# Tile shapes of the scores, the experts' results and the long turns, and the planner's booking of loads, in a fused attention and expert kernel

## The chip, the cores and the metric

One core of one Trainium2 chip. The metric is the time of one execution on the device in microseconds. Three executions of the kernel before took 511.32, 512.01 and 514.26 us (median 512.01); the profiled execution took 510.98 us, with 509.2 us from its first to its last instruction.

## What is computed

Two layers, all in float32. The first is attention with a window of 32 around each local query plus 32 global keys, and 32 global queries that see every key; 8 batches, 8 heads, 512 local and 32 global positions, head size 64. Cut to its core:

```python
s_g   = scale * q_g @ concat(k_g, k_l).T ;  out_g = softmax(s_g) @ concat(v_g, v_l)
s_ll  = where(|i - j| <= 32, scale * q_l @ k_l.T, -1e9)
out_l = softmax(concat(scale * q_l @ k_g.T, s_ll)) @ concat(v_g, v_l)
x     = concat(out_g, out_l), heads side by side          # [8, 544, 512]
```

The second is four causal attention "experts" on x, each of width 64, of which every position takes the two with the largest logits, weighted:

```python
logits = x @ w_gate ; top 2 of 4, softmax over the two -> gate
for e in range(4):
    q, k, v = x @ wq[e], x @ wk[e], x @ wv[e]
    out += gate[e] * (softmax(causal(scale * q @ k.T)) @ v @ wo[e])
```

## The kernel before, in words

Work comes in 32 pairs of heads (8 batches of 4 pairs). For a pair, `p1_load` and `p1_load_values` fetch keys, queries and values; `p1_trans` turns keys and queries (for the first four pairs by TensorE, line 523, afterwards on VectorE, lines 533 to 536) into `kd` and `qp`; GpSimd copies values into window order (`move`, lines 480 to 500, recorded at line 277) and the global keys into `kd` (line 515). `p1_scores` (line 553) takes local scores: 32 products on tiles of 64 rows and 32 columns, one PSUM bank per half of the rows. `p1_softmax` (565, 568) follows, `p1_ptrans` turns the probabilities, `p1_av` (616) multiplies with values on 128x32 tiles, `p1_turn` turns the result into x. For two pairs together `p1_global_scores` (678) takes the 32 global queries of four heads against all keys, on 128x64 tiles: the queries of two heads stand in a block-diagonal buffer (`qgbd`, cleared at the start), so that all 128 rows hold one product. `p1_global_turn` turns the probabilities, `p1_global_av` (731) multiplies.

Per batch come the projections `m_qk` (761) and `m_v` (798, 809) on full 128x128 tiles, the gates, and for each of two pairs of experts `c`: `m_scores` (890) on 64x64 tiles in three blocks of 384, 384 and 512 columns, `m_softmax` (904, 908, 922), `m_ptrans`, and `m_av` (957) on 128x64 tiles; `m_out` (1037) multiplies with wo. The last 32 positions, the "tail", of all four experts go together: `m_tail_scores` (979) on 128x64 tiles with a block-diagonal `qtbd`, `m_tail_turn`, `m_tail_av` (1018).

Two ways of turning stand in the code. `turn_halves` (586) turns a block as two tiles of 64 rows and 128 columns, each half into a bank of its own, and copies each bank out with one copy. `long_turn` (709), for the global and the tail probabilities, turns whole 128x128 blocks: four blocks into one bank, then a fifth into another, with two or three copies out.

A product of float32 operands is recorded as two matmul instructions (32 products of line 553 are 64 instructions); turns and products of float32r operands are one.

The order is not written out: `step(s)` lists the operations of a step with a priority of 100 s, and `Plan.place` simulates the engines with the costs that each `op` names and emits the instructions in that simulated order. Each engine then runs its own list in order. On TensorE the planner takes, of the ready operations within 130 of the lowest priority, the one with the smallest start time + 300 ns if its `shape` label differs from the last one's + 4 ns per unit of priority; the labels are local, quarter (expert scores), half (global and tail scores, experts' results), av, turn, and none for full tiles. A load books 700 ns and its own transfer time on one simulated DMA clock and counts as landed 1100 ns later; at most 8 loads are under way. These times exist only in the planner: on the chip an instruction waits for its data and its buffer alone. Loads are issued from SP's queue, and at priorities under 100 from ScalarE's too.

In `step`, the local part (`local`) follows the turns from step 6 on; global scores come earlier in the step, after the products with values; tail scores follow the first experts' results; long turns are spread among the full-tile products by `whole`. `setup(kind)` loads the weights of a kind (line 393 on) and splits them on VectorE (405, 407); values' weights at step 1.

## Time and profile before

| | before |
|---|---|
| executions, us | 511.32, 512.01, 514.26 |
| profiled execution, us | 510.98 |
| its span, us | 509.2 |
| TensorE busy, us (share) | 477.3 (94%) |
| TensorE weight loads, us | 405.2 (80%) |
| VectorE busy, us | 393.4 (77%) |
| ScalarE busy, us | 329.7 (65%) |
| GpSimd busy, us | 283.8 (56%) |
| instructions | 23800, of them 9564 matmuls |
| mean granted clock of TensorE | 0.989 |

Busy time is the time in which an engine had at least one instruction under way; matmuls overlap, so the time that a block takes on TensorE is read from its start to the start of the next block, not from a mean duration. The granted clock is the share of 2.4 GHz that TensorE was given.

### The profile page before, as it was taken

The numbers are of one execution on the slowest core, as the hardware profiler recorded it, in microseconds if no ns is written. First come the engines' busy times: TensorE is split into PE (matmuls) and PEld (weight loads), VectorE is DVE, ScalarE is ACT, GpSimd is POOL, SyncE is SP. The second block draws the span as 40 slices with busy tenths as digits, with TensorE's granted clock in tenths as the row PEclk, the third lists the DMA queues.
The fourth block names the chain that finished last, engine by engine and source line by source line (L and its number), as shares of the span: only waits on it lengthen the run. The fifth ranks groups of instructions, "written<-read, shape, count | busy, mean of one in ns | idle before, by whom it ended". The sixth has DMA issues, their size and how long they took to land.

```text
span 509.2 us, 23800 instructions
## 1 busy us (share of the span) xinstructions
PE 477.3 (94%) x9564; PEld 405.2 (80%) x9564; DVE 393.4 (77%) x1738; ACT 329.7 (65%) x1208; POOL 283.8 (56%) x521
## 2 busy tenths in 40 slices
PE   5687789999999998999999999999999999999995
PEld 3566778698877897789887898789886988889764
DVE  7697788997968896598987797598986797476480
ACT  1687357876957566595867666686768683553562
POOL 7886967878365673748358481838529220431220
PEclk9799899999999999999999999999999999999999
DMA  9977786443344513553243612644222000200102
GB/s 183 169 132 143 123 151 123 93 82 73 63 94 123 104 24 61 139 91 71 45 94 111 124 21 43 171 88 86 45 53 84 4 3 3 85 1 2 68 19 103
DMA packets 190190, 41.92 MB, mean 82 GB/s; under 512 B 185472, under 2 KB 185472, under 8 KB 190080
## 3 DMA queue, kind: packets, MB, share of 16 engines
q1 hardware_dynamic: 179040, 30.00, 32.6%
q10 hardware_dynamic: 11040, 10.41, 6.5%
q8 instruction: 75, 1.23, 1.1%
q14 instruction: 35, 0.29, 0.2%
HBM read 31.47 MB, written 8.91 MB: 79 GB/s over the span
## 4 chain that ended last, share of the span: by engine, by line
PE 76%; POOL 7%; DVE 6%; DMA 6%; issue 3%; ACT 2%; ACTq 1%; SPq 0%; POOLq 0%; DVEq 0%
PE bank L761 18%; PE bank L586 8%; PE bank L798 8%; PE bank L890 7%; PE bank L1037 7%; PE bank L957 6%; PE bank L553 5%; PE bank L616 5%; POOL v L277 5%; PE bank L678 3%; DMA v<-in_v_l_dram 2%; PE bank L709 2%; PE bank L731 2%; DMA kn<-in_k_l_dram 2%; PE bank L809 2%
## 5 line engine op out<-in xcount | busy, mean ns | idle before, releaser
L922 POOL TENSOR_SCALAR pm<-pm,msm,gate 128x512 f32<-128x512 f32 (+3 forms) x125 | 75.0, 614 | 115.1 <-DVE msm L913 63.9
L277 POOL COPY v<-v 32x512 f32<-32x512 f32 (+1 forms) x192 | 116.9, 609 | 31.7 <-DMA v<-in_v_l_dram 22.4
L568 ACT ACTIVATE st<-st,sm 128x128 f32<-128x128 f32 x256 | 99.3, 391 | 12.7 <-DVE sm L565 12.4
L277 POOL COPY v<-vg 32x640 f32<-32x640 f32 (+1 forms) x96 | 65.2, 680 | 45.7 <-PE bank L731 33.2
L908 ACT ACTIVATE pm<-pm,msm 128x512 f32<-128x512 f32 (+3 forms) x128 | 70.8, 555 | 16.3 <-DVE msm L904 14.0
L904 DVE CUSTOM_DVE_ANT_0 pm<-bank,cmask 128x512 f32<-128x512 f32 (+3 forms) x128 | 56.0, 483 | 12.8 <-PE bank L890 11.6
L565 DVE CUSTOM_DVE_ANT_0 st<-bank,band 128x128 f32<-128x128 f32 x256 | 56.9, 280 | 0.1
L568 ACT ACTIVATION_READ_ACCUMULATOR st<-st,sm 128x1 f32 x256 | 48.4, 189 | 0.0
L890 PE MATMUL bank<-kt,qt 64*64 64x384 f32 (+3 forms) x512 | 42.7, 442 | 0.8 <-issue 0.4
L553 PEld LDWEIGHTS bank<-kd,qp 64*32 64x32 f32 x2048 | 29.5, 107 | 17.5 <-issue 5.5
L553 PE MATMUL bank<-kd,qp 64*32 64x128 f32 x2048 | 39.1, 278 | 0.9 <-issue 0.7
L761 PE MATMUL bank<-xh,wk_hi 128*128 128x272 f32 x128 | 39.1, 305 | 0.3 <-DVE xn L620 0.2
L957 PE MATMUL bank<-mptw,vt 128*64 128x128 f32 x640 | 39.1, 275 | 0.2 <-DVE mptw L277 0.2
L798 PE MATMUL bank<-wv_hi,xl 128*128 128x260 f32 x128 | 36.3, 283 | 2.2 <-DVE xl L654 2.2
L761 PE MATMUL bank<-xh,wq_hi 128*128 128x272 f32 x128 | 38.1, 298 | 0.0
L798 PE MATMUL bank<-wv_hi,xh 128*128 128x260 f32 x128 | 37.4, 292 | 0.0
L761 PE MATMUL bank<-xl,wk_hi 128*128 128x272 f32 x128 | 37.3, 291 | 0.0
L761 PE MATMUL bank<-xh,wk_lo 128*128 128x272 f32 x128 | 37.3, 291 | 0.0
L761 PE MATMUL bank<-xl,wq_hi 128*128 128x272 f32 x128 | 36.9, 288 | 0.0
L761 PE MATMUL bank<-xh,wq_lo 128*128 128x272 f32 x128 | 36.9, 288 | 0.0
L957 PEld LDWEIGHTS bank<-mptw,vt 128*64 128x64 f32 x640 | 35.2, 137 | 1.9 <-issue 0.6
L616 PE MATMUL bank<-v,ptw 128*32 128x64 f32 x2048 | 35.9, 221 | 0.5 <-ACT ptw L275 0.3
(164 smaller groups left out, 1301.7 us busy)
## 6 DMA issues: line engine op xcount, KB each, us to landing
out_dram<-ot ACTq DMA_DIRECT2D x32, 256.0 KB, 2.1
v<-in_v_l_dram SPq DMA_DIRECT2D x62, 120.0 KB, 3.0
kn<-in_k_l_dram SPq DMA_DIRECT2D x112, 64.0 KB, 2.5
qn<-in_q_l_dram SPq DMA_DIRECT2D x112, 64.0 KB, 2.5
v<-in_v_l_dram SPq DMA_DIRECT2D x30, 64.0 KB, 3.1
vg<-in_v_g_dram SPq DMA_DIRECT2D x22, 64.0 KB, 2.9
kn<-in_k_l_dram SPq DMA_DIRECT2D x5, 128.0 KB, 4.0
ot<-in_q_g_dram SPq DMA_DIRECT2D x8, 64.0 KB, 2.5
```

The source lines that it names most:

```text
L277: ENG[e].tensor_copy(out, in_)
L553: nc.tensor.matmul(sp[h].t[32 * g:32 * g + 32, 128 * t:128 * t + 128], qp.t[rows, 32 * u:32 * u + 32], kd.t[rows, c:c + 128], start=True, ...
L565: op("DVE", 211, lambda e, h=h, t=t, i=i: nc.vector.tensor_tensor_reduce(out=st.t[:, h, t], in0=sp[h].t[:, 128 * t:128 * t + 128], in1=ban ...
L568: op("ACT", 385, lambda e, h=h, t=t, i=i: nc.scalar.activation(st.t[:, h, t], st.t[:, h, t], AF.Exp, bias=sm.t[:, 0, i:i + 1], scale=-1.0, ...
L616: nc.tensor.matmul(xq.t[32 * g:32 * g + 32, t, h, :], pt.t[:, h, 32 * u:32 * u + 32], v.t[:, h, window(u), :], start=True, stop=True)
L761: nc.tensor.matmul(pp.t, w[:, ch, cols], x(part, ch)[:, n], start=(ch == 0 and w is hi and part == 0), stop=(ch == NCH - 1 and part == 1))
L798: nc.tensor.matmul(pv.t, x(part, ch)[:, 128 * i:128 * i + 128], w[:, ch, :], start=(ch == 0 and part == 0 and w is hi), stop=(ch == NCH - ...
L890: nc.tensor.matmul(sp[x].t[64 * u:64 * u + 64, at:at + n], qt.t[rows, q0:q0 + 64], kt.t[rows, :n], start=True, stop=True)
L904: op("DVE", 78 + 1.04 * n, lambda e, x=x, at=at, n=n, i=i, s=s: nc.vector.tensor_tensor_reduce(out=pm.t[:, x, at:at + n], in0=sp[x].t[:, a ...
L908: op("ACT", 280 + 0.83 * n, lambda e, x=x, at=at, n=n, s=s: nc.scalar.activation(pm.t[:, x, at:at + n], pm.t[:, x, at:at + n], AF.Exp, bia ...
L922: lambda e, x=x, at=at, n=n, i=i, s=s: ENG[e].tensor_scalar(pm.t[:, x, at:at + n], pm.t[:, x, at:at + n], sm.t[:, 3, s:s + 1], gate.t[:, i ...
L957: nc.tensor.matmul(yp.t[64 * x:64 * x + 64, 128 * i - n0:128 * i - n0 + 128], vt.t[:, j, 64 * (2 * c + x):64 * (2 * c + x) + 64], flat[:, ...
```

## The change

Expert scores, global scores and tail scores are cut into tiles of 64 rows and 32 columns, with the label "scores" that local scores get too; experts' results into tiles of 128 rows and 32 columns, with the label "av". Queries of global rows and of the tail are read in place, so the block-diagonal buffers, their clears and the copies into them go. Long turns become one call of `turn_halves` on five blocks, into two banks, with two copies out; they stand among the turns of the step instead of among the full-tile products. Tail scores and global scores move to the head of the local part. In the planner a load may start only when at most 2000 ns of transfers are booked ahead, and it counts as landed 1600 ns after its transfer instead of 1100. The weights of values are set up a step later, and the first half of each weight's split may go to ScalarE. The diff, cut to its core:

```diff
 LANES = 8
+AHEAD = 2000.0
+LAND = 1600.0
...
-                        t = max(t, lanes[0])
+                        t = max(t, lanes[0], dma - AHEAD)
                     s = self.slot_time(o.bufs)
...
                 dma = max(dma, end + 700.0) + o.packets
-                seen = dma + 1100.0
+                seen = dma + LAND
                 lanes = lanes[1:] + [seen]
...
-    qgbd = []
-    for i in range(2):
-        t = const.tile([128, NP, 64], F32, name=f"qgbd{i}")
-        nc.vector.memset(t, 0.0)
-        qgbd.append(t)
-    qg_ring = Ring(2, fixed=qgbd)
-
-    qtbd = []
-    for i in range(2):
-        t = const.tile([128, 2, 64], F32, name=f"qtbd{i}")
-        nc.vector.memset(t, 0.0)
-        qtbd.append(t)
-    qt_ring = Ring(2, fixed=qtbd)
-
-
     def window(u):
...
         for cut, part, n in parts:
-            op("DVE", 100 + 0.6 * n, lambda e, cut=cut, part=part: nc.vector.tensor_copy(cut(hi), part()), r=[raw],
+            op("ACT|DVE", (150 + 0.83 * n, 100 + 0.6 * n), lambda e, cut=cut, part=part: copy(e, cut(hi), part()), r=[raw],
                w=[("w", kind)])
...
         op("PE", 390, f, r=[gn], w=[pg], shape="turn")
-        kg = buf("kg", [128, NP, SG])
-        qb = Buf(qg_ring)
-        evac(lambda: kg.t, lambda: pg.t[:, :, :32], 128, [pg], [kg])
-        for h in range(2):
-            rows = slice(64 * h, 64 * h + 64)
-            evac(lambda rows=rows, h=h: qb.t[rows, :, 32 * h:32 * h + 32], lambda rows=rows: pg.t[rows, :, 32:], 128,
-                 [pg], [(qb, h)])
-        G[b].update(kg=kg, qb=qb)
+        kq = G[b]["kq"] = buf("kq", [128, NP, 2 * SG])
+        evac(lambda: kq.t, lambda: pg.t, 256, [pg], [kq])
...
         pr = PR[k]
-        kg = G[b]["kg"]
+        kq = G[b]["kq"]
         kn, qn = pr["kn"], pr["qn"]
...
         op("POOL", 380, lambda e: nc.gpsimd.tensor_copy(
-            groups(kd.t)[:, :, 96:], kg.t[:, p:p + 1, :].to_broadcast([128, n3, SG])), r=[kg], w=[(kd, "g")])
+            groups(kd.t)[:, :, 96:], kq.t[:, p:p + 1, :SG].to_broadcast([128, n3, SG])), r=[kq], w=[(kd, "g")])
         if k < FIRST:
...
                                          start=True, stop=True)
-        op("PE", 990, f, r=[qp, kd], w=sp, shape="local")
+        op("PE", 990, f, r=[qp, kd], w=sp, shape="scores")
...
-        qb = G[b]["qb"]
+        kq = G[b]["kq"]
         sg = buf("long", [128, 640])
...
             def f(e, half=half, sp=sp):
-                for j in range(2):
-                    p, kd, o_ = 2 * g + j, kdl[j].t, sp.t[64 * j:64 * j + 64]
-                    if half == 0:
-                        parts = [(o_[:, :128], kd[:, :128]),
-                                 (o_[:, 128:].rearrange("p (c s) -> p c s", s=96),
-                                  kd[:, 128:512].rearrange("p (c s) -> p c s", s=128)[:, :, :96])]
-                    else:
-                        parts = [(o_[:, :96], kd[:, 512:608]), (o_[:, 96:], kd[:, 640:])]
-                    for to, k_ in parts:
-                        nc.tensor.matmul(to, qb.t[:, p, :], k_, start=True, stop=True)
-            op("PE", 754 - 520 * half, f, r=[qb, *kdl], w=[sp], shape="half")
+                for k in range(2):
+                    for j in range(2):
+                        for h in range(2):
+                            rows = slice(64 * h, 64 * h + 64)
+                            kd, o_ = kdl[j].t[rows], sp.t[64 * j + 32 * h:64 * j + 32 * h + 32]
+                            if half == 0:
+                                to, k_ = [(o_[:, :128], kd[:, :128]),
+                                          (o_[:, 128:].rearrange("p (c s) -> p c s", s=96),
+                                           kd[:, 128:512].rearrange("p (c s) -> p c s", s=128)[:, :, :96])][k]
+                            else:
+                                to, k_ = [(o_[:, :96], kd[:, 512:608]), (o_[:, 96:], kd[:, 640:])][k]
+                            nc.tensor.matmul(to, kq.t[rows, 2 * g + j, SG:], k_, start=True, stop=True)
+            op("PE", 754 - 520 * half, f, r=[kq, *kdl], w=[sp], shape="scores")
             op("DVE", 78 + 1.04 * n, lambda e, sp=sp, half=half, n=n: nc.vector.tensor_scalar(
...
-    def long_turn(src, key, where, part, chunks):
-
-        some = chunks[4:] if part else chunks[:4]
-        n = len(some)
-        pa = ps([128, n, 128], "pga")
-        if part == 0:
-            where[key] = buf("longt", [128, 5, 128])
-        pt = where[key]
-
-        def f(e):
-            for j, (at, rows) in enumerate(some):
-                nc.tensor.transpose(pa.t[:rows, j, :], src.t[:, at:at + rows], ident)
-        op("PE", 110 * n, f, r=[src], w=[pa])
-        rows = min(rows for _, rows in some)
-        evac(lambda: pt.t[:rows, 4 * part:4 * part + n, :], lambda: pa.t[:rows], 128 * n, [pa], [(pt, part)])
-        if rows < 128:
-            evac(lambda: pt.t[rows:, 0, :], lambda: pa.t[rows:, 0, :], 128, [pa], [(pt, "g")])
-
-    def p1_global_turn(b, g, part):
-        long_turn(G[b, g]["sg"], "pt", G[b, g], part, CHUNKS)
+    def long_turn(src, key, where, starts):
+
+        pt = where[key] = buf("longt", [128, 5, 128])
+        turn_halves([lambda at=at: src.t[:, at:at + 128] for at in starts], [src], into(lambda: pt.t, pt, 5))
+
+    def p1_global_turn(b, g):
+        long_turn(G[b, g]["sg"], "pt", G[b, g], [at for at, _ in CHUNKS])
...
         evac(lambda: t.t[:, n], lambda: pp.t, HS, [pp], [(t, half)])
-        if kind == "q" and half == 1:
-            if c == 0:
-                M[b, "qt"] = Buf(qt_ring)
-            qt = M[b, "qt"]
-            for x_ in range(2):
-                rows = slice(64 * x_, 64 * x_ + 64)
-                evac(lambda rows=rows, x_=x_: qt.t[rows, c, 32 * x_:32 * x_ + 32],
-                     lambda rows=rows: pp.t[rows, HS - SG:], 32, [pp], [(qt, (c, x_))])
...
                 n = 128 * (i + 1)
-                for u in range(2):
+                for u in range(4):
                     for x in range(2):
                         rows = slice(64 * x, 64 * x + 64)
-                        q0 = 128 * i + 64 * u
-                        nc.tensor.matmul(sp[x].t[64 * u:64 * u + 64, at:at + n], qt.t[rows, q0:q0 + 64],
+                        q0 = 128 * i + 32 * u
+                        nc.tensor.matmul(sp[x].t[32 * u:32 * u + 32, at:at + n], qt.t[rows, q0:q0 + 32],
                                          kt.t[rows, :n], start=True, stop=True)
-        op("PE", 80 + 1.67 * sum(128 * (i + 1) for i, _ in TILES[t]), f, r=[kt, qt], w=sp, shape="quarter")
+        op("PE", 80 + 1.67 * sum(128 * (i + 1) for i, _ in TILES[t]), f, r=[kt, qt], w=sp, shape="scores")
...
                     for j in range(i + 1):
-                        for x in range(2):
-                            nc.tensor.matmul(yp.t[64 * x:64 * x + 64, 128 * i - n0:128 * i - n0 + 128],
-                                             vt.t[:, j, 64 * (2 * c + x):64 * (2 * c + x) + 64],
-                                             flat[:, where[x, i, j], :], start=(j == 0), stop=(j == i))
+                        for d in range(4):
+                            nc.tensor.matmul(yp.t[32 * d:32 * d + 32, 128 * i - n0:128 * i - n0 + 128],
+                                             vt.t[:, j, 128 * c + 32 * d:128 * c + 32 * d + 32],
+                                             flat[:, where[d // 2, i, j], :], start=(j == 0), stop=(j == i))
             op("PE", 214 * sum(i + 1 for i in some), f, r=[vt, *{id(pts[i][0]): pts[i][0] for i in some}.values()], w=[yp],
-               shape="half")
+               shape="av")
             high_low(lambda part, n0=n0, n=n: y[part].t[:, c, n0:n0 + n], lambda yp=yp: yp.t, n, [yp],
...
     def m_tail_scores(b):
-        qt = M[b, "qt"]
         gt = M[b, "gt"]
         kts = [M[b, c, "k"] for c in range(2)]
+        qts = [M[b, c, "q"] for c in range(2)]
         pm = buf("long", [128, 640])
...
             def f(e, n0=n0, n=n, sp=sp):
-                for c in range(2):
-                    nc.tensor.matmul(sp.t[64 * c:64 * c + 64], qt.t[:, c, :], kts[c].t[:, n0:n0 + n], start=True, stop=True)
-            op("PE", 30 + 1.67 * n, f, r=[qt, *kts], w=[sp], shape="half")
+                for z in range(E):
+                    c, rows = z // 2, slice(64 * (z % 2), 64 * (z % 2) + 64)
+                    nc.tensor.matmul(sp.t[32 * z:32 * z + 32], qts[c].t[rows, SL:], kts[c].t[rows, n0:n0 + n],
+                                     start=True, stop=True)
+            op("PE", 30 + 1.67 * n, f, r=[*qts, *kts], w=[sp], shape="scores")
             if half == 0:
...
-    def m_tail_turn(b, part):
-        long_turn(M[b, "ptail"], (b, "pttail"), M, part, [(128 * j, 128) for j in range(5)])
+    def m_tail_turn(b):
+        long_turn(M[b, "ptail"], (b, "pttail"), M, [128 * j for j in range(5)])
...
         def local():
+            if r == 1 and has(old):
+                m_tail_scores(old)
+            if at(s) and s % 2 == 1:
+                bb, p = PAIRS[s]
+                p1_global_scores(bb, p // 2)
             if at(s):
...
                 whole_turns.append(M[old, "turn"])
-        if at(s) and s % 2 == 1:
-            bb, p = PAIRS[s]
-            p1_global_scores(bb, p // 2)
         if r == 1 and has(old):
             m_av(old, 0)
-            m_tail_scores(old)
         if r == 3 and has(old):
...
             turns.append(lambda: sooner(s - 2, p1_turn))
+        if at(s - 1) and s % 2 == 0:
+            turns.append(lambda: p1_global_turn(PAIRS[s - 1][0], PAIRS[s - 1][1] // 2))
+        if r == 2 and has(old):
+            turns.append(lambda: m_tail_turn(old))
         if at(s + 1):
...
-        if at(s - 1) and s % 2 == 0:
-            bb, p = PAIRS[s - 1]
-            whole_turns += [lambda: p1_global_turn(bb, p // 2, 0), lambda: p1_global_turn(bb, p // 2, 1)]
-        if r == 2 and has(old):
-            whole_turns += [lambda: m_tail_turn(old, 0), lambda: m_tail_turn(old, 1)]
         if s == LAG - 1:
...
         step(s)
-        for name, when in (("masks", 3), ("v", 1), ("k", 3), ("q", 4), ("o", 6)):
+        for name, when in (("masks", 3), ("v", 2), ("k", 3), ("q", 4), ("o", 6)):
             if s == when:
```

## Rows read from the trace of the kernel before

**Rows 1.** Busy time of each engine by stretch of the span, with instruction counts

```profile
0.00:12.73 12.73, 6.53 (x97) 4.69 (x99) 9.16 (x45) 2.33 (x6) 9.18 (x31) 1.00 1.11 183
12.73:25.46 12.73, 8.82 (x188) 7.07 (x193) 7.98 (x48) 7.70 (x34) 11.32 (x19) 0.73 0.97 169
25.46:38.20 12.74, 11.09 (x431) 8.49 (x419) 12.70 (x60) 11.05 (x49) 10.89 (x21) 1.00 0.70 132
38.20:76.40 38.20, 30.99 (x687) 27.77 (x688) 30.08 (x123) 20.21 (x83) 28.37 (x46) 0.96 0.79 139
76.40:490.00 413.60, 406.89 (x8043) 347.11 (x8041) 328.40 (x1451) 281.51 (x1024) 221.88 (x404) 1.00 0.33 70
490.00:509.20 19.20, 13.00 (x140) 10.11 (x140) 5.04 (x16) 6.85 (x17) 2.16 (x4) 0.97 0.20 69
```

**Rows 2.** Timeline of TensorE at the head of one batch

```profile
212.32 1.53 PE L890 MATMUL bank<-kt,qt 64*64 64x128 f32 x24
213.77 1.16 PE L553 MATMUL bank<-kd,qp 64*32 64x128 f32 x64
214.86 1.10 PE L616 MATMUL bank<-v,ptw 128*32 128x64 f32 x64
215.89 1.09 PE L890 MATMUL bank<-kt,qt 64*64 64x512 f32 x8
216.91 1.16 PE L553 MATMUL bank<-kd,qp 64*32 64x128 f32 x64
```

**Rows 3.** Timeline of TensorE, middle of the same batch

```profile
224.49 0.71 PE L586 MATMUL bank<-ident,st 64*128 64x64 f32 x16
225.04 0.91 PE L586 MATMUL bank<-ident,pm 64*128 64x64 f32 x24
225.79 0.41 PE L586 MATMUL bank<-ident,xn 64*128 64x64 f32 x8
...
226.62 1.10 PE L616 MATMUL bank<-v,ptw 128*32 128x64 f32 x64
227.54 0.75 PE L731 MATMUL bank<-v,longt 128*32 128x64 f32 x40
228.22 1.23 PE L678 MATMUL bank<-kd,qgbd 128*64 128x128 f32 x16
229.22 2.43 PE L957 MATMUL bank<-mptw,vt 128*64 128x128 f32 x40
231.44 1.17 PE L979 MATMUL bank<-kt,qtbd 128*64 128x512 f32 x8
232.53 0.71 PE L586 MATMUL bank<-ident,st 64*128 64x64 f32 x16
```

**Rows 4.** Timeline of TensorE, the first block of the next batch

```profile
270.48 0.88 PE L890 MATMUL bank<-kt,qt 64*64 64x384 f32 x8
```

**Rows 5.** Timeline of TensorE, a long turn between other blocks

```profile
247.22 0.66 PE L709 MATMUL bank<-ident,long 128*128 128x128 f32 x4
247.63 0.37 PE L761 MATMUL bank<-xh,wk_hi 128*128 128x272 f32 x1
```

**Rows 6.** Instructions on the tile of tail queries: ns least, median, most

```profile
L275 ACT COPY qtbd<-bank x25: 178/180/181, 66.6 to 471.8; 64x32 f32<-64x32 f32 x25
```

**Rows 7.** Timeline of TensorE at the start, waits in brackets

```profile
13.34 0.66 PE L523 MATMUL bank<-ident,kn 128*128 128x128 f32 x4 [0.31 <-DMA kn<-in_k_l_dram]
17.59 1.09 PE L523 MATMUL bank<-ident,qn 128*128 128x128 f32 x4 [3.60 <-DMA qn<-in_q_l_dram]
18.61 1.96 PE L553 MATMUL bank<-kd,qp 64*32 64x128 f32 x64
...
47.93 0.39 PE L798 MATMUL bank<-wv_hi,xh 128*128 128x260 f32 x1
```

**Rows 8.** Timeline of ScalarE's queue at the start

```profile
9.77 2.15 ACTq L293 DMA_DIRECT2D qn<-in_q_l_dram  x2
```

**Rows 9.** Timeline of VectorE at the start

```profile
25.18 0.68 DVE L405 CAST wv_hi<-mptw 128x1024 fp32r<-128x1024 f32 x1
```

## The prediction

> **What bounds the kernel now.** I read the busy time by stretch first, then TensorE's own order in one batch, then the start. TensorE is busy 477.3 of 509.2 us, and by stretch the kernel has three parts [rows 1]. From 76.40 to 490.00 TensorE is busy 406.89 of 413.60 us, so only 6.7 us of that stretch is waiting: whatever shortens TensorE's own work there shortens the kernel almost one for one. Up to 76.40 it is idle for 6.2, 3.9, 1.7 and 7.2 us of the four stretches, 19.0 us together, and there the chain of loads, copies and softmax decides. The last 19.20 us hold 13.00 us of TensorE and a drain of results. The other engines leave room after 76.40 (VectorE 328.40 of 413.60), but not before: from 25.46 to 38.20 VectorE has 12.70 of 12.74 us.
>
> In the middle the reader should look at what a change of tile shape costs. The local values' product (line 616, 128x32 tiles) takes 0.92 us to the next start where a product of the same shape follows (226.62 to 227.54), and 1.03 us where expert scores on 64x64 tiles follow (214.86 to 215.89) [rows 2, 3]. The instructions are the same 64, so the change of shape costs 0.11 us. Whole products lose about as much; I take 0.105 us a change. In the batch from 212.32 to 270.48 I count 25 changes of shape [rows 2, 4]; 7.1 such batches of 58.16 us fill the 413.60 us.
>
> **The change part by part, against the profiled execution's own 510.98 us** (its span 509.2; the median of the three runs is 1.0 us higher, far inside what I leave open).
>
> *Fewer shapes.* Expert scores (line 890), global scores (678) and tail scores (979) take the local scores' 64x32; experts' results (957) take the values' 128x32. In the batch of the rows, four pairs of neighbours become one shape: expert scores and the local scores behind them (212.32 with 213.77, and 215.89 with the next at 216.91, twice per batch). The two runs of 128x64 (global scores, experts' results, tail scores, 228.22 to 232.53) dissolve: the results join the products of values ahead of them, and the global and tail scores, now issued in the step's local part, join a run of scores. That is 6 of 25. 7.1 x 6 would be 43; the first and last batches hold fewer such neighbours, and relabelling every block in the order after 76.40 this way, long turns put among the other turns, removes 39: 39 x 0.105 = 4.1 us. With fewer classes the planner, which pays 300 ns in its cost for a change, can regroup once more per batch: 7 batches x 0.105 = 0.7 us. Bounds: 20 x 0.105 = 2.1 us (only the expert/local pairs) to 55 x 0.105 = 5.8 us.
>
> *Twice the instructions in these blocks.* Expert scores stream the same columns on eight tiles instead of four. The nearest rows: local scores stream 4 x 128 columns by 64 instructions in 1.09 us (213.77 to 214.86), expert scores 512 columns by 8 in 1.02 us (215.89 to 216.91) [rows 2]; 56 more instructions add 0.07 us, 1.25 ns each. The change adds at most 24 to a block (24 to 48), so 0.03 us; 48 blocks of (8 batches, 2 pairs of experts, 3 tiles) would add 0.5 us with 8 each as the least. I take +0.5, bounds 0 to 48 x 0.07 = 3.4. Experts' results take 2.22 us for 40 instructions (229.22 to 231.44) [rows 3], 0.055 us each, two side by side; four side by side on 128x32 need 80 instructions, and line 616 starts one in 0.92/64 = 0.014 us, so 1.15 us of issue lies under 2.22 us of streaming: 0, bounds 0 to 16 x 40 x 1.25 ns = 0.8 us. Global and tail scores get the same treatment: 0, if the rival below doesn't hold.
>
> *Long turns in row halves.* Now four blocks in 0.41 us (247.22 to 247.63) [rows 5] and the fifth by itself, hardly more than its issue. After: ten instructions of the row-half turns, of which 24 take 0.75 us (225.04 to 225.79) and 16 take 0.55 us (224.49 to 225.04) [rows 3], so 0.31 to 0.34 us. Of the 24 (two per batch for global rows, one for the tail) some 20 lie after 76.40: at the 0.06 us between the lower of these and the middle, 20 x 0.06 = 1.2 us off TensorE, if they sit in a run of turns; at worst each opens a run of its own, +2.1. Their evacuations go from three copies (two for the tail) to two of 320 columns. The 32 copies into the masked tail queries go (25 on ScalarE at 0.18 us, so 5.8 us in all [rows 6]), as do two of three copies per batch turn and four clears at the start. I count all that as 0 after 76.40, where both engines wait for TensorE; were they the bound there, the 5.8 us would be worth half of it each.
>
> *Loads.* The two new numbers enter only the planner's clock (a load waits there until no more than 2 us of transfers are booked; landing is taken 0.5 us later). No instruction waits for them on the chip: they alter the order on SP's and ScalarE's queues and, through the expected landings, TensorE's order. What the order of before does wrong is visible: line 523 turns pair 2's keys at 13.34, then waits 3.60 us for pair 2's queries, and pair 1's local scores, whose keys and queries had been turned already, stand behind it until 18.61 [rows 7]. The late transfer was issued from ScalarE's queue between 9.77 and 11.92 [rows 8], behind values. The scores then show 1.96 us instead of the 1.16 of the same 64 instructions at 213.77: the granted clock of that stretch is 0.73 [rows 1, 2, 7], part of it on the 1.2 GHz level, after this idle time. With values held back and landings expected later, pair 1's scores should go ahead of that turn. Value weights move a step (some 6 us) later, past pair 4's keys and queries and pair 3's values on SP, which so come a weight's issue earlier; the weights are wanted at 47.93 [rows 7] and their first cast stands at 25.18 [rows 9], so the delay lies under over 15 us of other work; without that cover it would cost its 6 us. Casts that may go to ScalarE relieve VectorE just where it is full. Of the 19 us idle before 76.40 I take -3.0 us: the 3.6 us wait, less what VectorE keeps. Bounds: -6 (wait, slow clock and part of VectorE's queue) to +3 (another load late in its turn).
>
> *New waits.* The row-half long turn needs two PSUM banks at once, where it had one; global and tail scores stand earlier in their step, and in TensorE's fixed order everything queues behind a block whose keys or banks are late; softmax on VectorE and ScalarE waits behind that. The middle has 6.7 us of waits now. I take +1.0, bounds -1 to +4.
>
> Sum: 510.98 - 4.1 - 0.7 + 0.5 - 1.2 - 3.0 + 1.0 = 503.5; toward the median of runs, **504.0 us**.
>
> **Rivals.**
> *Row halves in one bank take turns (slower).* Global and tail scores had all 128 rows in one tile; now rows 0 to 63 and 64 to 127 are separate tiles that write into one bank, on different 32 partitions. In the kernel of before every helper that splits rows (local and expert scores, turns) gives each half a bank of its own, so no row shows this case. If the halves exclude each other, each block streams its columns twice: 16 global blocks by another 1.00 us (228.22 to 229.22) and 8 tail blocks by another 1.0 (231.44 to 232.53 without the change) [rows 3], +24 us, giving 528. It decides from the point where 8 of these 24 blocks double. Against it: the partitions are disjoint, and the four column groups already run side by side in line 616. Chance 0.10. The Trainium skill bears on this: "TensorEngine Tiling (Array Packing)", Gotcha 1 (PSUM Pressure), says that different row tiles cannot access one PSUM bank at the same time, and does not say whether different partitions are exempt. By that rule the sum is the 528 of this rival; no run here shows it yet.
>
> *The order hardly changes.* The planner may keep scores apart because their banks or inputs come at different times, and the start may stay: -2.1 - 1.2 + 0.5 + 0.5 from the middle and 0 from the start give 508.7, with new waits up to 512. For it: two runs of scores with a run of values between them (212.32 to 215.89) already serve one step each. Chance 0.16.
>
> *The start moves as a whole.* Pair 1's softmax five us earlier pulls pairs 2 to 5 along, -6: 501, or 498 with the low ends of the middle. Against it: VectorE is full from 25.46 to 38.20. Chance 0.10.
>
> *New waits at their upper bound with a late load:* 504 + 3 + 6 = 513, chance 0.02 slower, 0.02 the same.
>
> **How the numbers follow.** The forecast has 0.60 with 499 to 508 of its own. A measurement of this kernel tells about 0.5% (2.6 us) from no change, so faster means below 509.4, slower above 514.6. Faster: 0.60 + 0.10 + 0.06 of the order rival = 0.76; same: 0.10 of it + 0.02 = 0.12; slower: 0.10 + 0.02 = 0.12. The range 496.5 to 511.5 leaves out the bank rival and the ends of the others.
>
> **What would show it.** Right: 64x32 scores back to back, about 17 to 19 changes of shape in a batch of about 57 us, TensorE still busy over 97% from 76 to 490; 0.3 us per long turn; pair 1's local scores before 15 us. Wrong: global scores at 2 us a block or second-half instructions that start only when the first half ends (bank rival); a middle stretch with over 10 us of idle TensorE; the same 3.6 us wait at line 523.

## The result, and the profile after

The change makes the kernel slower: 516.71 us median of 20 executions (512.45 to 520.71) against 512.28 us of 20 executions of the kernel before on the same chip, ratio 1.0075 with a 95% interval of 1.0053 to 1.0097. Ratios, here and below, are of fast executions alone, without two of the 20 here (520.18 and 520.71) that count as slow, so they are not quite those of the medians. The profiled execution took 519.15 us, 517.4 from first to last instruction, 8.2 us more than before. The forecast was 504.0.

The busy time by stretch, in the columns of [rows 1] (length, then busy time and instructions of TensorE, its weight loads, VectorE, ScalarE, GpSimd; granted clock, DMA share, GB/s):

```profile
0.00:12.73 12.73, 6.16 (x69) 4.66 (x77) 9.45 (x39) 1.84 (x3) 10.63 (x32) 1.00 1.02 176
12.73:25.46 12.73, 10.36 (x337) 8.68 (x322) 10.32 (x63) 9.88 (x43) 11.24 (x22) 1.00 0.82 149
25.46:38.20 12.74, 9.01 (x377) 6.90 (x365) 11.21 (x48) 9.26 (x41) 6.98 (x12) 1.00 0.64 123
38.20:76.40 38.20, 30.72 (x710) 27.56 (x711) 29.12 (x113) 19.92 (x77) 27.55 (x48) 0.82 0.85 149
76.40:490.00 413.60, 393.98 (x9328) 347.11 (x9335) 317.77 (x1414) 267.08 (x965) 223.69 (x405) 0.99 0.33 70
490.00:517.40 27.40, 20.08 (x373) 15.51 (x371) 11.87 (x45) 12.22 (x35) 3.47 (x6) 0.92 0.19 66
```

The fifth line decides. TensorE is idle for 413.60 - 393.98 = 19.6 us of that stretch, where it was idle for 6.7 [rows 1]. No other engine became the bound: VectorE and ScalarE are busy for 10.6 and 14.4 us less. What TensorE waited for in that stretch (total, times, longest):

```profile
PE bank L982 <- issue: 6.0, 3, 2.0
PE bank L919 <- issue: 4.4, 3, 2.1
PE bank L597 <- DVE msm L866: 2.9, 6, 0.6
PE bank L701 <- issue: 2.0, 2, 1.7
PE bank L597 <- issue: 1.4, 1, 1.4
PE bank L567 <- issue: 0.7, 2, 0.5
PE bank L534 <- issue: 0.6, 1, 0.6
PE bank L567 <- DVE msm L866: 0.6, 1, 0.6
PE bank L661 <- issue: 0.4, 1, 0.4
```

"issue" means that nothing in the profile released the instruction: no semaphore, engine or load. I call these untraced waits; here they are 15.5 us, in the kernel before 2.9, of which these are 2.4 (the other two are of 0.3 and 0.2 us):

```profile
PE bank L1018 <- issue: 1.5, 2, 1.4
...
PE bank L678 <- issue: 0.5, 1, 0.5
...
PE bank L890 <- issue: 0.4, 1, 0.4
```

They sit inside blocks, not between them. TensorE's timeline around one (start, length, line, tile, count; in brackets the idle time and what ended it):

```profile
200.27 1.19 PE L661 MATMUL bank<-kd,kq 64*32 64x128 f32 x32
202.06 1.10 PE L597 MATMUL bank<-v,ptw 128*32 128x64 f32 x64 [0.60 <-DVE msm L866]
202.95 0.77 PE L701 MATMUL bank<-v,longt 128*32 128x64 f32 x40
203.51 0.54 PE L982 MATMUL bank<-vt,longt 128*32 128x64 f32 x23
206.03 0.69 PE L982 MATMUL bank<-vt,longt 128*32 128x64 f32 x17 [1.98 <-issue]
206.47 3.82 PE L919 MATMUL bank<-mptw,vt 128*32 128x128 f32 x80
```

The tail's values (982) stop after 23 of their 40 products, for 1.98 us, with all their inputs there. Such a stop comes once in each of five batches, at 144, 204, 264, 324 and 384 us, in the run values (597), global values (701), tail values (982), experts' results (919): 64 + 40 + 40 + 80 products in a row (products are counted here and below as recorded, two for each float32 product). In the other half of a batch the run lacks the tail's 40, and it passes without a stop at 174, 234, 294 and 354 us (not at 116); the one at 294:

```profile
294.25 1.10 PE L597 MATMUL bank<-v,ptw 128*32 128x64 f32 x64 [0.46 <-DVE msm L866]
295.16 0.75 PE L701 MATMUL bank<-v,longt 128*32 128x64 f32 x40
295.73 2.37 PE L919 MATMUL bank<-mptw,vt 128*32 128x128 f32 x80
```

A stop costs more than itself when the clock falls behind it. The 80 products of line 919 take 3.82 us at 206.47 and 2.37 at 295.73; the granted clock right behind the stop (the third number from the end) is 0.50, the 1.2 GHz level:

```profile
206.03:209.20 3.17, 3.17 (x69) 3.17 (x72) 0.81 (x5) 0.40 (x2) 0.90 (x2) 0.50 0.67 149
```

After 76 us this happened behind two of the five stops (the second at 266.35, where line 919 took 3.58 us), some 1.3 us each. Behind the stop that ended at 146.59 the same block took 2.36, and why the clock fell behind some stops only is not shown.

What is late during such a stop is the instructions themselves. The third part of the page counts the transfers that bring them; queue 8, before and after:

```profile
q8 instruction: 75, 1.23, 1.1%
```

```profile
q8 instruction: 87, 1.43, 1.1%
```

1.43 MB in 87 packets is 16 KB a packet. TensorE ran 11156 products after and 9564 before, each with one weight load, 22312 and 19128 instructions; 87 x 256 = 22272 and 75 x 256 = 19200. So one packet is 256 of TensorE's instructions, 128 products with their loads, 64 bytes each. The Trainium skill gives that size too, in "Trainium Architecture — The Big Picture", section "The software stack"; that section has the streams carried into the engines when the program is loaded, while this trace shows TensorE's arriving throughout the run.

In the trace's transfers the packet ahead of the stop above starts at 203.14 and has landed at 204.69; the stop ends at 206.03. Each of the five long stops ends 1.3 to 1.5 us after a packet has landed. Counting products shows that this is no coincidence. From each of these stops to the next TensorE does 1402, 1402, 1402 and 1403 products, and 11 packets land each time, 11 x 128 = 1408. All untraced waits of 0.2 us and more behind the first 10 us, 15 in this trace and 157 in all 14 kept traces, stand on this grid: 128 products for each packet that has landed, plus a rest that only falls, from 88 near the start to 49 near the end in this trace (about 100 other instructions of TensorE stand in between). So each of them stands where the delivered products are used up and one more packet has just come in.

### The profile page after: what moved, and what is told of

Its sections match the earlier page's. It is cut to its first block, busy times and chain, and to the rows that moved or that the text cites. A ratio compares the mean times of both kernels' runs of the same rounds, so it can differ in the third digit from the quotient of the medians.

```text
span 517.4 us, 26911 instructions
## 1 busy us (share of the span) xinstructions
PE 470.3 (91%) x11156; PEld 410.4 (79%) x11156; DVE 389.7 (75%) x1718; ACT 320.2 (62%) x1160; POOL 283.6 (55%) x521
## 3 DMA queue, kind: packets, MB, share of 16 engines
q8 instruction: 87, 1.43, 1.1%
## 4 chain that ended last, share of the span: by engine, by line
PE 74%; DVE 8%; DMA 6%; issue 5%; SPq 4%; POOL 1%; ACT 1%; ACTq 1%; POOLq 0%; DVEq 0%
PE bank L731 18%; PE bank L567 9%; PE bank L1001 9%; PE bank L760 8%; PE bank L919 7%; PE bank L597 6%; PE bank L534 5%; PE bank L852 5%; SPq L295 4%; DMA v<-in_v_l_dram 2%; PE bank L701 2%; PE bank L661 2%; DVE pm L866 2%; DVE st L546 2%; PE bank L771 1%
## 5 line engine op out<-in xcount | busy, mean ns | idle before, releaser
L277 ACT COPY ptw<-bank 128x512 f32<-128x512 f32 x34 | 19.7, 587 | 51.0 <-PE bank L567 50.6
L919 PE MATMUL bank<-mptw,vt 128*32 128x128 f32 x1280 | 43.0, 288 | 4.5 <-issue 4.4
L534 PE MATMUL bank<-kd,qp 64*32 64x128 f32 x2048 | 41.4, 282 | 1.9 <-issue 1.1
L852 PE MATMUL bank<-kt,qt 64*32 64x384 f32 (+3 forms) x1024 | 42.9, 432 | 0.0
L919 PEld LDWEIGHTS bank<-mptw,vt 128*32 128x32 f32 x1280 | 38.1, 117 | 5.7 <-issue 5.5
L597 PEld LDWEIGHTS bank<-v,ptw 128*32 128x32 f32 x2048 | 31.4, 112 | 13.2 <-issue 7.8
L534 PEld LDWEIGHTS bank<-kd,qp 64*32 64x32 f32 x2048 | 32.6, 109 | 9.8 <-issue 4.5
L496 POOL COPY kd<-kq 128x160 f32<-128x160 f32 x32 | 10.2, 320 | 50.5 <-PE bank L661 25.5
L731 PE MATMUL bank<-xh,wk_hi 128*128 128x272 f32 x128 | 37.8, 296 | 0.0
```

The costliest lines, as they stand in the source:

```text
L534: nc.tensor.matmul(sp[h].t[32 * g:32 * g + 32, 128 * t:128 * t + 128], qp.t[rows, 32 * u:32 * u + 32], kd.t[rows, c:c + 128], start=True, ...
L597: nc.tensor.matmul(xq.t[32 * g:32 * g + 32, t, h, :], pt.t[:, h, 32 * u:32 * u + 32], v.t[:, h, window(u), :], start=True, stop=True)
L731: nc.tensor.matmul(pp.t, w[:, ch, cols], x(part, ch)[:, n], start=(ch == 0 and w is hi and part == 0), stop=(ch == NCH - 1 and part == 1))
L852: nc.tensor.matmul(sp[x].t[32 * u:32 * u + 32, at:at + n], qt.t[rows, q0:q0 + 32], kt.t[rows, :n], start=True, stop=True)
L919: nc.tensor.matmul(yp.t[32 * d:32 * d + 32, 128 * i - n0:128 * i - n0 + 128], vt.t[:, j, 128 * c + 32 * d:128 * c + 32 * d + 32], flat[:, ...
```

## The experiments

Two theories. **Supply:** TensorE's instructions come 128 products at a time, at a bounded pace; a stretch with more products than that stalls, so the change pays for the products it added, 512 in expert scores and 640 in experts' results. (320 more in global and tail scores and 120 in long turns make up the 1592; no run takes the 320 back.) **Start and order:** the load edits and the new places of the score blocks push the first product with the values' weights from 47.93 [rows 7] to 52.08 us, and all else follows; or a tile of 32 columns is by itself slower.

The table gives every kernel timed more than once beside the kernel before on the same chip, which was timed anew each time (medians 512.28, 511.62, 511.10 and 511.95 us; the last row has the first); the last column adds TensorE's untraced waits between 76.40 and 490.00 us from the view of waits shown above.

| kernel | median, us | ratio to before, 95% | untraced, us |
|---|---|---|---|
| the change | 516.71 | 1.0075, 1.0053 to 1.0097 | 15.5 |
| without its load edits | 515.07 | 1.0064, 1.0036 to 1.0091 | 12.7 |
| load edits alone | 510.13 | 0.9984, 0.9962 to 1.0007 | 4.9 |
| change, results on 64 columns | 511.91 | 0.9987, 0.9959 to 1.0016 | 9.7 |
| change, expert scores on 64 | 512.27 | 1.0000, 0.9965 to 1.0034 | 9.5 |
| change, both on 64 | 506.43 | 0.9903, 0.9865 to 0.9940 | 3.3 |
| both on 64, without load edits | 505.95 | 0.9895, 0.9849 to 0.9941 | 3.4 |
| both on 64, own labels | 517.24 | 1.0120, 1.0063 to 1.0177 | 8.4 |
| before, results on 32 | 517.35 | 1.0116, 1.0082 to 1.0150 | 6.5 |
| before, expert scores on 32 | 516.37 | 1.0095, 1.0060 to 1.0129 | 10.1 |
| before, score labels made one | 510.85 | 0.9977, 0.9953 to 1.0001 | 2.2 |
| before, long turns in halves | 511.74 | 1.0009, 0.9978 to 1.0040 | 7.3 |
| before | 512.28 | 1 | 2.9 |

**The two halves of the change.** The changed kernel without its load edits, and the kernel before with nothing but them (shown for the first; the cut hides the split of the weights, which goes back to VectorE alone):

```diff
-AHEAD = 2000.0
-LAND = 1600.0
+AHEAD = 1.0e9
+LAND = 1100.0
...
-        for name, when in (("masks", 3), ("v", 2), ("k", 3), ("q", 4), ("o", 6)):
+        for name, when in (("masks", 3), ("v", 1), ("k", 3), ("q", 4), ("o", 6)):
```

> The changed kernel with the four edits on loads undone (no bound on booked transfers, landing 1100 ns, value weights at step 1, splits on VectorE). Theory 'two losses': the late start of the changed kernel (first value projection at 52.1 against 47.9) comes from the loads, and TensorE's waits without a releaser ('issue', 15.3 us after 76 us against 2.4 before) come from the denser runs of short products. Then here the first value projection stands at 47 to 49 us, the issue waits stay at 10 to 16 us, and the time is 512 to 514 us. Rival 'the start alone': the middle's waits follow from the late start; then the time is 506 to 509 us with under 5 us of issue waits.

> The kernel before with the four edits on loads alone. Theory 'two losses': the weights of k land after their cast's turn on VectorE and hold it; the first value projection moves from 47.9 to 51 to 53 us and the time to 515 to 517 us, with issue waits as before (2 to 4 us after 76 us). Rival 'the loads gain': pair 1's local scores go at 15 instead of 18.6 us and nothing is lost later: 507 to 510 us.

The shapes alone are slower by 0.64%, nearly all of the loss, and their first product with the values' weights still comes at 52.15 us. The load edits alone are within 0.4% of no change, although there too this product stands at 52.14; by the first product with wo it has caught up (147.3 us, 148.0 before). I had expected the late start to come with the loads, and to cost; both were wrong. A start that is 4 us late at that point costs nothing that can be told from noise here, and the loss is in the shapes.

**One width at a time, same order.** In the changed kernel, with the planner's costs and labels and so the order of the blocks kept, the experts' results go back to 64 columns; then both blocks; then expert scores alone:

```diff
-                        for d in range(4):
-                            nc.tensor.matmul(yp.t[32 * d:32 * d + 32, 128 * i - n0:128 * i - n0 + 128],
-                                             vt.t[:, j, 128 * c + 32 * d:128 * c + 32 * d + 32],
+                        for x in range(2):
+                            nc.tensor.matmul(yp.t[64 * x:64 * x + 64, 128 * i - n0:128 * i - n0 + 128],
+                                             vt.t[:, j, 64 * (2 * c + x):64 * (2 * c + x) + 64],
...
-                for u in range(4):
+                for u in range(2):
                     for x in range(2):
                         rows = slice(64 * x, 64 * x + 64)
-                        q0 = 128 * i + 32 * u
+                        q0 = 128 * i + 64 * u
```

> The changed kernel, the same order of blocks on every engine, with the experts' results on 128x64 tiles again (the label stays av): 640 products and as many weight loads fewer. Theory 'supply of instructions': the five waits of 1.7 to 2.2 us in the runs values, global values, tail values, experts' results shrink or go, with the slow clock behind them; against that some 17 to 30 more changes of shape at 0.105 us. Issue waits after 76 us fall from 15 to under 8 us, the time to 507 to 512 us. Rival 'the waits are of banks or data': same order, same waits, 517 to 520 us.

> The changed kernel, the same order of blocks, with the experts' results on 128x64 and the expert scores on 64x64 tiles again, so with about as many instructions as before. Theory 'supply': issue waits after 76 us fall further, from the 9.8 us of the run with the results alone undone to 4 to 8 us; about 35 changes of shape come back (3.7 us), so the time is 510 to 514 us, no better than with the results alone undone. Rival 'only the results' blocks matter': issue waits stay at 9 to 10 us and the time is 514 to 517 us.

> The changed kernel in its own order with only the expert scores back on 64x64 (results stay on 128x32): the fourth corner of the square of widths. Supply theory: the stalls go with the number of instructions in the dense runs; the results' 80 products are the last straw of the run values, global values, tail values, results, so this keeps most stalls of 2 us: 511 to 515, untraced waits 8 to 13 us. Were expert scores by themselves the cause (each block of 48 running at half pace): 506 to 508, untraced waits under 5 us.

The four corners lie on a plane. From both on 32 (1.0075) the results' 64 columns give 0.88%, the scores' 0.75%, both 1.72%, that is 4.5, 3.8 and 8.8 us of 512; the untraced waits fall by 5.8, 6.0 and 12.2 us of the 15.5. Neither block alone is the cause: each pays for its products, wherever in the order the stop then falls. These are net prices: with 64 columns some 53 changes of shape after 76 us come back (137 and 190), 5.6 us at the prediction's 0.105, and the kernel is faster all the same. With both on 64 columns four untraced waits of that stretch are left (3.3 us, the longest 1.2), and this version beats both kernels, the one before by 1.0%. I had expected 510 to 514: the rest of the change is worth more than I thought.

**One width at a time, in the kernel before.** The same edits the other way, results on 128x32 in the order of before, and expert scores on 64x32 with the label of local scores. For the second, the last kernel shown here shares that label but leaves the tiles at 64x64, so its order is the same:

```diff
-        op("PE", 990, f, r=[qp, kd], w=sp, shape="local")
+        op("PE", 990, f, r=[qp, kd], w=sp, shape="scores")
...
-        op("PE", 80 + 1.67 * sum(128 * (i + 1) for i, _ in TILES[t]), f, r=[kt, qt], w=sp, shape="quarter")
+        op("PE", 80 + 1.67 * sum(128 * (i + 1) for i, _ in TILES[t]), f, r=[kt, qt], w=sp, shape="scores")
```

> The kernel before, the same order of blocks on every engine, with the experts' results on 128x32 tiles (the label stays half). Theory 'supply': the block itself stays at 2.2 to 2.3 us, but in the runs in which global scores stand right ahead of it the wait without a releaser grows: issue waits after 76 us from 2.4 to 4 to 9 us, time 513 to 518 us. Rival 'narrow tiles are slower in themselves': the block of 2.2 us takes 2.5 us or more everywhere, 16 x 0.3 = 5 us more, and issue waits stay at 2 to 3 us. Rival 'nothing': 510 to 513 us.

> The kernel before with the expert scores alone on 64x32 tiles, under one label with the local scores. It merges about 20 pairs of neighbours (-2.1 us) and adds 512 products with their loads of weights in the runs of scores. Theory 'supply': issue waits after 76 us rise from 2.4 to 4 to 8 us, nearly all within or just behind runs of scores, and the time is 511 to 515 us. Rival 'the number of instructions does not matter': waits stay at 2 to 3 us and the time is 508.5 to 510.5 us.

> The kernel before with the planner's label of expert scores and local scores made one, the tiles left at 64x64: the same order of blocks as with expert scores on 64x32 alone (516.37), 768 fewer pairs of load and product on half the number of tiles. Supply theory: the label alone is within 3 us of the kernel before, 508 to 513, and untraced waits after 76 us come back under 5 us from 10.0. If the order is what costs: 515 to 517 again, with untraced waits about as before.

640 more products in the results cost 1.16%, 5.9 us, and 3.6 us of untraced waits; 15 changes of shape more (186 and 201 after 76 us) would be another 1.6. The block's own time did not grow (2.32 us, start to start, against 2.21 plus the change of shape behind it). Expert scores on 32 columns are 0.95% slower though they save 37 changes of shape after 76 us; with the same labels and 64 columns the kernel is 0.23% faster than before, an interval that just reaches no change. The 512 products so cost 1.18%, 6.0 us, in an order that is otherwise the same. I had expected 4 to 8 us of untraced waits; they are 10.1 us against 2.2. The largest are these, first with 32 and then with 64 columns:

```profile
PE bank L1018 <- issue: 2.9, 2, 1.7
PE bank L616 <- issue: 2.3, 4, 1.5
PE bank L731 <- issue: 2.2, 3, 1.0
...
PE bank L553 <- issue: 1.2, 2, 0.7
...
PE bank L709 <- issue: 0.9, 1, 0.9
```

```profile
PE bank L731 <- issue: 1.3, 2, 1.0
...
PE bank L616 <- issue: 0.4, 1, 0.4
```

**The pace by itself.** The values' product of pairs 13 and 29 is run eight times over (timed once, 537.67 us), on the same inputs into the same bank (the last pass gives the result), in the kernel before. Nothing new is read, no block waits for another engine, and 512 products stand in a row:

```diff
-            for t in range(4):
+            for t in [x for _ in range(8 if k in (13, 29) else 1) for x in range(4)]:
...
-        op("PE", 825, f, r=[v, pt], w=[xq], shape="av")
+        op("PE", 6600 if k in (13, 29) else 825, f, r=[v, pt], w=[xq], shape="av")
```

> The kernel before with the product of local values done eight times over for pairs 13 and 29 (the same result is written again): 512 products and 512 loads of weights in one unbroken block without a new input. Theory 'supply': the block starts at 0.014 us per product as before and then falls to the pace of the fetches, 256 instructions per 3.3 to 4 us, 0.026 to 0.031 us per product, with gaps of 1 to 2.5 us that end 1 to 2 us after a fetch has landed; the block takes 11 to 16 us. Rival 'the waits are of data, banks or order': 8 x 0.92 = 7.3 to 7.6 us, without gaps.

TensorE's timeline over the first of the two, and then over the second:

```profile
170.49 2.92 PE L616 MATMUL bank<-v,ptw 128*32 128x64 f32 x193
175.03 1.99 PE L616 MATMUL bank<-v,ptw 128*32 128x64 f32 x128 [1.62 <-issue]
178.76 1.99 PE L616 MATMUL bank<-v,ptw 128*32 128x64 f32 x128 [1.74 <-issue]
182.22 1.04 PE L616 MATMUL bank<-v,ptw 128*32 128x64 f32 x60 [1.46 <-issue]
...
418.37 1.99 PE L616 MATMUL bank<-v,ptw 128*32 128x64 f32 x128 [0.37 <-issue]
422.39 2.54 PE L616 MATMUL bank<-v,ptw 128*32 128x64 f32 x128 [2.02 <-issue]
425.86 2.54 PE L616 MATMUL bank<-v,ptw 128*32 128x64 f32 x128 [0.93 <-issue]
429.33 0.89 PE L616 MATMUL bank<-v,ptw 128*32 128x64 f32 x49 [0.93 <-issue]
```

Nearly everything can be read here. Between two stops stand 128 products, one packet. The bursts start 3.73, 3.46, 4.02, 3.47 and 3.47 us apart: a product costs 27 to 31 ns when its instructions have to be brought, where one from the stock takes 0.92/64 = 14 ns [rows 3]. A slower clock inside a burst changes nothing: 128 products take 1.99 us or, where 0.50 is granted from 423.70 to 427.00, 2.54, and the stop takes the rest. The window from 171.50 to 184.00 has four instruction packets:

```profile
q8 instruction: 4, 0.07, 2.3%
```

They start at 172.14, 176.06, 179.85 and 183.33, so one is under way at a time, and their bytes use 2.3% of the DMA engines in that window. A full DMA is not what holds them; what does is not shown.

**Long turns alone.** The kernel before with long turns as row halves among the other turns:

> The kernel before with the long turns alone in row halves and among the turns. Ten instructions take the place of five per long turn, so the supply of instructions hardly changes. Theory 'supply': issue waits after 76 us stay at 2 to 4 us and the block of ten costs 0.31 to 0.34 us, so 509 to 511.5 us. Rival 'banks': two banks at once delay the score blocks, and the time is 513 us or more.

The turns do get shorter: all turns after the first product with wo take 45.0 us from start to start, 47.7 before. The time is the same (1.0009), and the untraced waits, which I had expected to stay at 2 to 4 us, are 7.3, 4.4 us more than before: 24 long turns have ten products instead of five, so 120 short ones more, in places where short ones already stand.

**Loads once more, and labels that fit.** From the best kernel the load edits are undone; and, in another, its two 64-column blocks get labels of their own, as the tiles really are:

```diff
-        op("PE", 80 + 1.67 * sum(128 * (i + 1) for i, _ in TILES[t]), f, r=[kt, qt], w=sp, shape="scores")
+        op("PE", 80 + 1.67 * sum(128 * (i + 1) for i, _ in TILES[t]), f, r=[kt, qt], w=sp, shape="quarter")
...
-               shape="av")
+               shape="half")
```

> The kernel with both experts' blocks on 64 columns (506.43) with the load edits undone (planner's two new numbers, weights of values a step later, casts to ScalarE). Loads neutral, as measured alone (0.998): 505.5 to 508.5. If the gain of 5 us against the kernel before comes from the loads together with the new places of the score blocks: 509 to 512.

> Both experts' blocks on 64 columns, with labels of their own again (64x64 scores and 128x64 results each a class), so the planner sees the changes of shape that there are. Shape-change price of 0.105 us: some 10 to 25 changes fewer than the 190 with the shared labels, so 504 to 506 if nothing else moves. Supply theory says only that untraced waits after 76 us stay under 5 us; if they do and the time is still over 508, the order of the changed kernel was worth something by itself.

Loads are neutral a third time (0.9895 and 0.9903). The second is a miss, and the most instructive one: with the same instructions in another order, with 19 changes of shape fewer after the first product with wo (136 and 155), the kernel is 2.2% slower. Its untraced waits are 8.4 us instead of 3.3, and other waits joined them:

```profile
PE bank L701 <- issue: 3.9, 4, 1.9
PE bank L567 <- DVE xn L601: 3.5, 4, 1.0
PE bank L919 <- issue: 2.6, 3, 1.3
PE bank L597 <- issue: 1.3, 2, 0.9
```

The longest stop, at 170.77 us, stands behind tail, global and local scores, values and 23 of the global values' 40 products in a row, all short. Untraced and other waits together grew by 7.0 us, of the 8.4 us between the two profiled executions. The number of instructions alone therefore does not decide; their order, and with it how many of them stand together, does too. The planner books a price for a change of shape and none for instructions.

## Why the prediction was wrong

The step that failed is "Twice the instructions in these blocks". It took the price of a product from runs that came out of the stock ("line 616 starts one in 0.92/64 = 0.014 us, so 1.15 us of issue lies under 2.22 us of streaming: 0", and 1.25 ns for each instruction more in the scores). Inside a block that was right: line 919 takes 2.37 us with 80 products and took 2.43 with 40 [rows 3]. What it left out is that products also have to arrive (the words on the kernel before have an instruction wait for its data and its buffer alone; it waits for its own arrival too), 128 per 3.5 us in a long run, and that the stop falls wherever the stock ends, mostly in someone else's block. The sum had +0.5 us; the square of widths measured 8.8 us for both blocks, net of the changes of shape that they save.

By the other steps:

- *Fewer shapes*: right in the count, and the price is not shown by itself. I counted 186 changes after 76 us before and 137 after, 49 fewer where the forecast had 39 and one per batch; at 0.105 us, 5.1 us. The shared label on unchanged tiles, with 10 changes fewer after the first product with wo (140 and 150), gained 1.2 us with an interval of 0 to 2.4.
- *Long turns*: right for the block, 0.32 us from its start to the next, forecast 0.31 to 0.34; the -1.2 for all of them was too small, they save 2.7 us where they stand alone:

```profile
227.63 0.48 PE L567 MATMUL bank<-ident,long 64*128 64x64 f32 x10
227.95 0.41 PE L419 MATMUL bank<-ident,ot 64*128 64x64 f32 x4
```

- *Loads*: the sign came, not from the loads, and the 3.0 us did not. Pair 1's local scores start at 14.86 us (18.61 before) and the wait of 3.60 us [rows 7] is gone; from there to 23 us the longest one for a load is 0.56. But with the load edits alone these scores still stand behind the turn of pair 2, at 17.88, and the wait shrinks to 0.98 us, while without the load edits they start at 13.67 and there is no such wait. That they came "before 15 us" is luck: the other half of the change moved them. The gain was given back at 38.90, where global scores wait 5.04 us for VectorE. The first three lines are of the change, the next two of the load edits alone, the last of the change without them:

```profile
14.86 0.30 PE L534 MATMUL bank<-kd,qp 64*32 64x128 f32 x2
...
18.79 0.43 PE L419 MATMUL bank<-ident,ot 64*128 64x64 f32 x4 [0.56 <-DMA ot<-in_q_g_dram]
...
43.94 1.61 PE L661 MATMUL bank<-kd,kq 64*32 64x128 f32 x16 [5.04 <-DVE xl L289]
```

```profile
17.33 0.63 PE L525 MATMUL bank<-ident,qn 128*128 128x128 f32 x4 [0.98 <-DMA qn<-in_q_l_dram]
17.88 1.16 PE L555 MATMUL bank<-kd,qp 64*32 64x128 f32 x64
```

```profile
13.70 1.14 PE L534 MATMUL bank<-kd,qp 64*32 64x128 f32 x62
```

TensorE's idle time up to 76.40 is 20.2 us, 19.0 before. "Value weights move a step (some 6 us) later" and "the delay lies under over 15 us of other work" held for those weights. It missed the keys' weights, which were now issued at 36.67 and landed at 42.41: their cast stands on VectorE ahead of the split (`xl`) that TensorE waits for.
- *New waits*: +1.0 us forecast, 12.9 us measured, nearly all of it untraced (15.5 against 2.9). The waits that I had in mind, for banks and keys, hardly grew: the rest of the idle time was 3.8 us and is 4.1.
- *Row halves in one bank* (the rival with 528 us): refuted. Global scores on row halves that share a bank take 1.19 us at 200.27, 1.23 before [rows 3]; the halves run side by side. The rule of the Trainium skill that spoke for this rival, "TensorEngine Tiling (Array Packing)", Gotcha 1, does not hold here for halves that write to different partitions of a bank.

So against 510.98: -5.1 for shapes, -2.7 for turns (from the run with turns alone), 0 for the start, +12.9 idle, and about +2.6 for the two stretches at the lower clock make 518.7; the profiled execution took 519.15. That these are so close is luck in part: the price of a shape is the prediction's own, and the idle time that grew by 1.2 us up to 76.40 and by 1.1 behind 490.00 is not in it. The rival "new waits and a late load" (513, 0.02) had the sign and another mechanism. My own list named "a middle stretch with over 10 us of idle TensorE" as what would prove the forecast wrong, and that is what came.

**Open.** What bounds the pace of a packet per 3.5 us. In the run with the values eight times over it is made of 1.0 to 1.6 us from a burst's first product to the start of the next packet, 0.9 to 1.4 us of transfer and 1.2 to 1.6 us from landing to the next burst; in no trace do two packets overlap. How large the stock is can only be estimated: by the count of products above, never more than 270 products were there when a packet had just landed, so about two packets. And where exactly the best kernel's 1.0% comes from: loads are excluded, and by the sums of block times after the first product with wo it saves, among others, 4.4 us in turns and 2.1 in the projections, and it pays 3.6 more in experts' results. Of that, 2.6 are two blocks of 3.62 us instead of 2.33: the one at 201.21 holds a stop of 1.03 us, the one at 488.20 runs at a granted clock of 0.50. No run takes these apart.

## What to carry to other kernels

Before cutting a product into more tiles, count instructions per microsecond over the run of blocks around it, not in the block alone: here TensorE gets 128 recorded products with their weight loads per 3.5 us, 27 ns each, and a run that uses them in 14 to 20 ns lives on a stock of some 260. Waits that the profile puts down to nothing, in the middle of a block, together with the packet count of the instruction queue, point to it; products counted from one such wait to the next, against the packets that landed, settle it. Where short blocks must be, long ones between them should help: the same instructions in two orders were 2.2% apart, though no run here made an order to that end.

## What the runs showed that I had not expected

- TensorE's instructions arrive during the run in packets of 16 KB (87 in 517 us), and stops of 1.7 to 2.2 us follow when a run of short products outlasts them. All 157 untraced waits of 0.2 us and more in the 14 traces, behind the first 10 us, stand where a packet's products end.
- Behind two of the five stops the granted clock was halved (0.50 from 206.03 to 209.20), which made them dearer by about 1.3 us each; behind other stops of that length it was not.
- The early start of pair 1's local scores, which the prediction gave to the loads, came without the load edits too.
- The same instructions in an order with fewer changes of shape took 517.24 instead of 506.43 us.
